# One core, AdaLN block with FNet and gMLP: modulation columns by VectorE products and ScalarE row sums, the small DFT matrices folded later, the first rows of y in two halves

## The chip, the core and the metric

The kernel runs on one core of a Trainium2 chip. The metric is the device time in microseconds of one launch, and lower is better. TensorE (PE in the profile), VectorE (DVE), ScalarE (ACT), GpSimd (POOL) and SyncE (SP) each take their own instructions in program order. Here SP issues nearly all loads, and POOL issues the stores, some small transfers and the loads of x for the residual.

## What is computed

```python
x = A_x                                             # 2048 x 512
mod = (_silu(c) @ w_mod).reshape(c.shape[0], 6, 1, -1)   # c: 1 x 512, w_mod: 512 x 3072
sa, ca, ga, sb, cb, gb = ...                        # six rows of 512
h = _layernorm(x, axis=-1) * (1 + ca) + sa
a = h @ dft_hid_re.T ; b = h @ dft_hid_im.T         # 512 x 512 matrices
x = x + ga * (dft_seq_re @ a - dft_seq_im @ b)      # 2048 x 2048 matrices
h = _layernorm(x, axis=-1) * (1 + cb) + sb
x = x + gb * _B_ref(h, ...)                         # gelu, layernorm, w_sp (2048 x 2048), w_out
```

All is float32. The change touches only the first half, up to the first writes of the new x.

## The kernel before

**Matmuls in three.** Each float32 product is made of three reduced-precision matmuls (`matmul3`, L83): a high part by a high part, a low part by the high one, and the high one by a low part. ACT makes a high part by a copy, DVE makes the low part by a subtraction.

**Stage A.** The kernel does not form `a` and `b`. It multiplies the two sequence matrices by the normalised x first, and the small hidden matrices (called ht) afterwards, with the modulation folded into them. Stage A runs over 128 chunks, here called steps n. One step is 128 columns of 512 rows of a sequence matrix, against one tile s of 128 normalised rows of x: 12 matmuls of 128x512 (`mm_a`, L342). In quarter t = 0 the steps alternate in fours between the real matrix (j = 0) and the imaginary one (j = 1), so that tile s = 4 is first used at step 8, s = 8 at step 16 and s = 12 at step 24. Quarter 0 ends with step 31.

**The order of the work.** A table made with `at(n, function, ...)` says which extra work is emitted behind step n (L627 to L720). Each step is emitted as `prep(n)` (L151), `mm_a(n)`, and then the extra work in the order in which it was entered. `prep(n)` has DVE transpose chunk n+3 (tile `t`, L147), ACT copy its high part (`ah`, L170), and DVE make the low part of chunk n+2 (`al`, L179). There are two buffers of `t`, four of `ah` and three of `al`. So `al` of chunk n+2 waits until PE has finished step n-1, and DVE cannot run more than about two steps ahead of PE. A block of a sequence matrix (tile `stage`, 1 MB, four steps) is loaded by SP into one of two buffers.

**Normalising x.** Tiles 0 to 3 have their statistics from DVE (`stats_x`). For tiles 4 to 15 ACT sums a row (`sum_x`, L302), sums the squares at the next step (`square_x`, L307) and normalises at the one after (`norm_x`, L108), with small POOL operations on the sums between (L303, L308 to L310). `hi_h` (ACT, tile `hh`, L325) and `lo_h` (DVE, tile `hl`, L330) split the result one step later. `norm_x` also writes ones into the first column by a small ACT copy (L317).

**Folding the modulation.** Three things are needed from the modulation in stage A: the shift sa and the scale 1 + ca as columns (512 numbers over partitions), and ga as a row (`mod2`). For the columns, w_mod is loaded (`wm`, `load_mod`); POOL multiplies and adds its four pieces (`weigh_mod`, L228, L230); DVE transposes and reduces (`turn_mod` L236, `column_mod` L241); POOL writes the result to DRAM and reads it back in four pieces (L243, L247). The folding then takes, for each of the two ht matrices: a load (`load_ht`, tile `hraw`), four transposes (`turn_ht`), POOL products and sums with the shift column (`weigh_ht`, L385 and L387), a first row that goes through DRAM to be spread over partitions (`load_w0`, L375 and L377, `scale_w0` L380), a scaling (`fold_ht` L403), and the split (`make_ht`, `make_ht_lo`). All this sits between steps 1 and 40.

**Rows of y.** `mm_y(t, i)` (L421) multiplies 128 rows of the result of stage A by ht: 24 matmuls. For quarter 0 it runs behind steps 44, 45, 46 and 46; `post_y` (L430) applies `mod2`, adds x, stores and takes the statistics.

Of the kernel before, what the change touches and what calls it, by code (L numbers as in the profile page):

```python
# [8 lines left out]
F32 = mybir.dt.float32  # L9
# [10 lines left out]
def fnet_gmlp_kernel(  # L20
# [50 lines left out]
    def bank(k, name):  # L71
        return psum.tile([P, 512], F32, tag=f"bank{k}", bufs=1, name=name)
# [131 lines left out]
    def load_mod(j):  # L204
        if j < 3:
            wm[j] = [spool.tile([P, D], F32, tag=f"wm{k}", bufs=1, name=f"wm{j}_{k}") for k in range(ND)]
        else:
            w = hpre.tile([P, ND, D], F32, tag="hraw", bufs=1, name=f"wm{j}")
            wm[j] = [w[:, k, :] for k in range(ND)]
        for k in range(ND):  # L210
            nc.sync.dma_start(wm[j][k], w_mod[k * P:(k + 1) * P, j * D:(j + 1) * D])
# [13 lines left out]

    def weigh_mod(j, k):
        w = wm[j]
        nc.gpsimd.tensor_scalar(w[k], w[k], sc[:, k:k + 1], 1.0, op0=ALU.mult, op1=ALU.mult)  # L228
        if k:
            nc.gpsimd.tensor_tensor(w[0], w[0], w[k], op=ALU.add)  # L230

    part, COL = {}, {}

    def turn_mod(j):
        part[j] = rows.tile([P, D], F32, tag="row", bufs=6, name=f"part{j}").rearrange("p (b i) -> p b i", i=32)
        nc.vector.transpose(part[j], wm.pop(j)[0].rearrange("p (b i) -> p b i", i=32))  # L236

    def column_mod(j):

        some = spool.tile([P, 16], F32, tag="some", bufs=2, name=f"some{j}")  # L240
        nc.vector.reduce_sum(some, part.pop(j), axis=mybir.AxisListType.X)  # L241
        d = dram.tile([P, 16], F32, name=f"some_d{j}")
        nc.gpsimd.dma_start(d, some)  # L243
        four = htpool.tile([P, 5, 4], F32, name=f"four{j}")
        v = d.rearrange("(c i) (a k) -> a i c k", i=32, k=4)
        for a in range(4):
            nc.gpsimd.dma_start(four[32 * a:32 * a + 32, :4, :], v[a])  # L247
        if j:
            nc.gpsimd.dma_start(four[:, 4, :], d.rearrange("(c i) b -> i b c", i=32)[0, 0].partition_broadcast(P))
        COL[j] = four  # L250

    def add_columns(j):
        four = COL[j]
        col = COL[j] = htpool.tile([P, 5], F32, name=f"col{j}")
        nc.vector.reduce_sum(col[:, :4], four[:, :4, :].rearrange("p c k -> p k c"), axis=mybir.AxisListType.X)
        if j:
            nc.vector.reduce_sum(col[:, 4:5], four[:, 4:5, :], axis=mybir.AxisListType.X)
            nc.vector.tensor_scalar(col, col, 1.0, None, op0=ALU.add)
            COL[2] = htpool.tile([P, 5], F32, name="col2")
            nc.vector.tensor_scalar(COL[2], col, -1.0, None, op0=ALU.mult)  # L260

# [6 lines left out]
    def split_mod(j):  # L268
        w = wm[j][0]
        wm[j] = [rows.tile([P, D], F32R, tag="row", bufs=6, name=f"ws{j}_{i}") if j == 2 else  # L270
                 hpre.tile([P, D], F32R, tag=f"ht{1 + i}", bufs=1, name=f"ws{j}_{i}") for i in range(2)]
        split(*wm[j], w)
# [40 lines left out]
    def norm_x(s):  # L313
        if s not in LN:
            LN[s] = spool.tile([P, D], F32, tag="xn", bufs=4, name=f"xn{s}")
        apply(LN[s], X.pop(s), NRM.pop(s))
        nc.scalar.activation(LN[s][:, 0:1], ones[:, 0:1], AF.Copy)  # L317

# [4 lines left out]
    def hi_h(s):  # L323
        h_hi[s] = hpool.tile([P, ND, P], F32R, name=f"hh{s}")
        nc.scalar.activation(*parts_h(s, h_hi), AF.Copy)  # L325

    def lo_h(s):
# [3 lines left out]
        LN.pop(s)  # L331

    def split_h(s):
        hi_h(s)
        lo_h(s)

# [34 lines left out]
    W0, ACC, QP = {}, {}, {}  # L371

    def load_w0(j):

        nc.gpsimd.dma_start(hrow_d[j], HR[j, 0][0:1, :])  # L375
# [3 lines left out]
    def scale_w0(j):  # L379
        nc.vector.tensor_scalar(W0[j], W0[j], COL[1 + j][:, 4:5], None, op0=ALU.mult)  # L380
# [30 lines left out]

    def make_ht_lo(j, k, eng=nc.vector):
        ht_lo[j, k] = htpool.tile([P, D], F32R, name=f"htl{j}_{k}")
        eng.tensor_tensor(ht_lo[j, k], HR.pop((j, k)), ht_hi[j, k].bitcast(F32), op=ALU.subtract)

# [4 lines left out]

    def mm_y(t, i):  # L421
        ps = YP[t, i] = bank(6 + i % 2, f"yp{t}_{i}")
        for j in range(2):
            for k in range(ND):
                gh, gl = gt_hi[t, j, k], gt_lo[t, j, k]
                cols = slice(i * P, (i + 1) * P)
                matmul3(ps, gh[:, cols], gl[:, cols], ht_hi[j, k], ht_lo[j, k],
                        j == 0 and k == 0, j == 1 and k == ND - 1)

    def post_y(t, i):  # L430
        x2 = X[t, i]
        y = rows.tile([P, D], F32, tag="y", bufs=1, name=f"y{t}_{i}")
        nc.vector.tensor_tensor(y, YP.pop((t, i)), mods[2], op=ALU.mult)
        nc.vector.tensor_tensor(x2, y, x2, op=ALU.add)  # L434
        nc.gpsimd.dma_start(x2_d[t][i * P:(i + 1) * P, :], x2)  # L435
        NRM[t, i] = norm([x2], "y")
# [192 lines left out]
    at(1, lo_h, 3)  # L629
    at(1, load_mod, 1)  # L630
    at(4, load_x, 2)
    at(12, load_x, 3)
    begin = [2, 3, 4, 5, 9, 10, 12, 13, 16, 18, 20, 21]
    for s, n in zip(range(4, NS), begin):
        at(n, sum_x, s)
        at(n + 1, square_x, s)
        at(n + 2, norm_x, s)
        at(n + 3, split_h, s)
    for k in range(ND):
        at((6, 7, 8, 9)[k], weigh_mod, 1, k)  # L640
        at((13, 14, 15, 16)[k], weigh_mod, 0, k)
        at((12, 13, 14, 15)[k], turn_ht, 0, k)
        at((22, 23, 24, 24)[k], weigh_ht, 0, k)
        at((25, 25, 26, 26)[k], fold_ht, 0, k)
    at(10, turn_mod, 1)
    at(11, column_mod, 1)
    at(10, load_mod, 0)
    at(11, load_ht, 0)
    at(15, add_columns, 1)
    at(16, load_w0, 0)  # L650
    at(16, load_ht, 1)
    at(17, turn_mod, 0)
    at(18, column_mod, 0)
    at(18, load_mod, 2)
    at(20, scale_w0, 0)
    at(21, add_columns, 0)
    at(23, sum_mod, 2, [0, 1])
    at(24, sum_mod, 2, [2, 3])
    at(25, split_mod, 2)

# [6 lines left out]
    at(26, change_pools)  # L667
    at(26, split_acc, 0)
    at(29, spread_mod, 2, 3, htpool, False)
    at(30, spread_acc, 0, 2)  # L670
    at(30, row_ht, 0)
    for i, k in enumerate((1, 2, 3, 0)):
        n = (26, 27, 28, 31)[i]
        at(n, make_ht, 0, k)
        at(n + 1, make_ht_lo, 0, k)
    for k in range(ND):
        at((29, 29, 30, 30)[k], turn_ht, 1, k)
        at((30, 31, 32, 33)[k], weigh_ht, 1, k)
        at((34, 35, 35, 36)[k], fold_ht, 1, k)
    at(30, load_w0, 1)  # L680
    at(33, scale_w0, 1)
    at(34, split_acc, 1)
    at(36, spread_acc, 1, 7)
    at(36, row_ht, 1)
    for i, k in enumerate((1, 2, 3, 0)):
        n = (36, 37, 38, 39)[i]
        at(n, make_ht, 1, k)
        at(n + 1, make_ht_lo, 1, k, nc.gpsimd if k else nc.vector)
    at(42, load_mod, 4)
    for j, n, k, plus_one in ((4, 48, 6, True), (3, 56, 7, False), (5, 64, 6, False)):  # L690
        at(n, sum_mod, j, [0, 1])
        at(n + 1, sum_mod, j, [2, 3])
        at(n + 2, split_mod, j)
        at(n + 4, spread_mod, j, k, cpool if j == 5 else htpool, plus_one)
        if j < 5:
            at(n + 4, load_mod, 5 if j == 3 else 3)
    for t in range(NQ):
        n = 8 * NQ * (t + 1)
        for i in range(4):
            y = N2 - 1 if t == NQ - 1 else (44, 45, 46, 46)[i] if t == 0 else n + 1 + 3 * i  # L700
            if i < 2:
                at(y - 4, load_xr, t, i)
# [152 lines left out]
```

## Time and profile before

| | |
|---|---|
| time, median of 3 runs (lowest to highest) | 1021.5 us (1020.74 to 1021.58) |
| the profiled execution: its time, and its span | 1021.03 us, 1019.2 us |
| TensorE clock granted over the span | 0.992 of full |
| busy: PE, weight loads, DVE, ACT, POOL | 98%, 80%, 53%, 31%, 18% |
| DMA | 114.85 MB, mean 113 GB/s |

The span runs from the first to the last instruction of the program; the time holds 1.8 us more. All places in the trace are microseconds from the start of the span. A matmul's duration overlaps the next one's, so PE's rate is read from the number of matmuls in a stretch. Step 0 of stage A begins at 11.25 us, and its last step ends at about 458 us.

### The profile page before, as it was taken

The page shows a single profiled execution, that of the slowest core. Times are in us where ns is not written, and L with a number is a line of the kernel's source. Part 1 is how long each engine was busy: PE and PEld are TensorE (multiplying, and loading weights), DVE is VectorE, ACT ScalarE, POOL GpSimd, SP SyncE. Part 2 cuts the span into 40 slices and gives each one's busy share as a digit, 9 for nine tenths or more (in the row PEclk, how much of TensorE's full clock was granted, in tenths as well). Part 3 has the DMA queues.
Part 4 walks back from the last instruction along what each step waited for, and adds up shares of the span by engine and source line. Part 5 has one row for each costly group of instructions (what it writes and reads, how often), then busy time and mean ns, then how long its engine had stood idle before and what let it go on. Part 6 is the DMA issues. An engine that isn't in the chain of part 4 may idle for free.

```text
span 1019.2 us, 11695 instructions
## 1 busy us (share of the span) xinstructions
PE 995.1 (98%) x4346; PEld 820.3 (80%) x4346; DVE 535.6 (53%) x800; ACT 313.5 (31%) x518; POOL 186.3 (18%) x316
## 2 busy tenths in 40 slices
PE   8977899999999999999999999999999999999998
PEld 5865688788888888888888999888888888888886
DVE  6664984578455554655543477555332532262325
ACT  5745441233132321331444477421111111111101
POOL 2654351104220032103312111101100200020002
PEclk9988999999999999999999999999999999999999
DMA  9985364266535443673745223324424322522131
GB/s 208 211 172 123 85 142 115 77 151 176 133 104 124 83 95 99 137 149 93 211 147 197 73 42 70 85 84 124 110 66 128 79 62 63 155 52 62 42 135 42
DMA packets 146538, 114.85 MB, mean 113 GB/s; under 512 B 7440, under 2 KB 126256, under 8 KB 146480
## 3 DMA queue, kind: packets, MB, share of 16 engines
q1 hardware_dynamic: 139296, 93.61, 39.4%
q0 software_dynamic: 6656, 20.49, 5.8%
q8 instruction: 34, 0.56, 0.3%
q14 instruction: 24, 0.20, 0.1%
q10 hardware_dynamic: 528, 0.00, 0.0%
HBM read 94.13 MB, written 19.94 MB: 112 GB/s over the span
## 4 chain that ended last, share of the span: by engine, by line
PE 87%; DVE 4%; DMA 3%; ACT 2%; POOL 2%; issue 1%; SPq 1%; DVEq 0%; ACTq 0%; POOLq 0%
PE gw L84 10%; PE gw L86 10%; PE gw L85 10%; PE gp L85 9%; PE gp L86 8%; PE gp L84 8%; PE yp L85 3%; PE yp L84 3%; PE yp L86 3%; PE z2p L85 3%; PE z2p L84 3%; PE z2p L86 3%; PE z1p L84 2%; PE z1p L85 2%; PE z1p L86 2%; PE op L86 2%
## 5 line engine op out<-in xcount | busy, mean ns | idle before, releaser
L170 ACT ACTIVATE ah<-t 128x512 fp32r<-128x512 f32 x224 | 141.4, 631 | 551.3 <-PE gw L86 214.2
L179 DVE TENSOR_TENSOR al<-t,ah 128x512 fp32r<-128x512 f32 x224 | 158.5, 708 | 270.5 <-PE gw L85 140.2
L85 PE MATMUL gp<-al,hh 128*128 128x512 f32 x512 | 203.2, 397 | 14.3 <-DVE al L179 14.3
L84 PE MATMUL gp<-ah,hh 128*128 128x512 f32 x512 | 202.4, 395 | 4.2 <-ACT ah L170 4.2
L86 PE MATMUL gp<-ah,hl 128*128 128x512 f32 x512 | 201.9, 394 | 0.1
L86 PE MATMUL gw<-ah,zl 128*128 128x512 f32 x448 | 174.3, 389 | 0.0
L85 PE MATMUL gw<-al,zh 128*128 128x512 f32 x448 | 174.3, 389 | 0.0
L84 PE MATMUL gw<-ah,zh 128*128 128x512 f32 x448 | 174.3, 389 | 0.0
L147 DVE STREAM_TRANSPOSE t<-stage 128x512 f32<-128x512 f32 x208 | 146.4, 704 | 7.3 <-DMA stage<-in_A_dft_seq_re_dram 4.3
L85 PEld LDWEIGHTS gp<-al,hh 128*128 128x128 f32 x512 | 97.7, 191 | 38.7 <-DVE al L179 18.5
L84 PEld LDWEIGHTS gp<-ah,hh 128*128 128x128 f32 x512 | 97.5, 190 | 26.6 <-ACT ah L170 5.5
L86 PEld LDWEIGHTS gp<-ah,hl 128*128 128x128 f32 x512 | 97.8, 191 | 21.2 <-DVE hl L330 0.8
L86 PEld LDWEIGHTS gw<-ah,zl 128*128 128x128 f32 x448 | 84.1, 188 | 17.6
L85 PEld LDWEIGHTS gw<-al,zh 128*128 128x128 f32 x448 | 84.1, 188 | 17.5
L84 PEld LDWEIGHTS gw<-ah,zh 128*128 128x128 f32 x448 | 84.1, 188 | 17.3
L564 POOL TENSOR_TENSOR u<-u,g 128x512 f32<-128x512 f32 x16 | 21.4, 1339 | 336.1 <-DVE g L562 336.1
L84 PE MATMUL yp<-hth,gh 128*128 128x512 f32 x128 | 50.6, 395 | 0.0
L85 PE MATMUL yp<-htl,gh 128*128 128x512 f32 x128 | 50.6, 395 | 0.0
L86 PE MATMUL yp<-hth,gl 128*128 128x512 f32 x128 | 50.5, 394 | 0.0
L435 POOL DMA_DIRECT2D x_d<-xr x16 | 8.8, 548 | 211.9 <-DVE xr L434 211.7
L85 PE MATMUL z2p<-wil,ah 128*128 128x448 f32 x128 | 46.7, 365 | 0.0
L84 PE MATMUL z2p<-wih,ah 128*128 128x448 f32 x128 | 46.7, 365 | 0.0
(127 smaller groups left out, 1197.2 us busy)
## 6 DMA issues: line engine op xcount, KB each, us to landing
stage<-in_A_dft_seq_re_dram SPq DMA_DIRECT2D x64, 256.0 KB, 4.8
stage<-in_A_dft_seq_im_dram SPq DMA_DIRECT2D x64, 256.0 KB, 5.3
stage<-in_B_w_sp_dram SPq DMA_DIRECT2D x64, 256.0 KB, 4.8
stage<-h_d SPq DMA_DIRECT2D x32, 256.0 KB, 4.6
z_d<-z POOLq DMA_DIRECT2D x28, 256.0 KB, 5.9
u<-z_d SPq DMA_DIRECT2D x4, 1792.0 KB, 8.0
wm<-in_w_mod_dram SPq DMA_DIRECT2D x24, 256.0 KB, 6.5
xr<-in_A_x_dram POOLq DMA_DIRECT2D x16, 256.0 KB, 3.5
```

The source lines that it names most:

```text
L84: nc.tensor.matmul(acc, ah, bh, start=first, stop=False)
L85: nc.tensor.matmul(acc, ah, bl, start=False, stop=False)
L86: nc.tensor.matmul(acc, al, bh, start=False, stop=last)
L147: nc.vector.transpose(dst.rearrange("p (b i) -> p b i", i=32), block[:, :, 32 * k:32 * k + 32])
L170: nc.scalar.activation(AH[n], T[n], AF.Copy)
L179: nc.vector.tensor_tensor(AL[n], T.pop(n), AH[n].bitcast(F32), op=ALU.subtract)
L435: nc.gpsimd.dma_start(x2_d[t][i * P:(i + 1) * P, :], x2)
L564: eng.tensor_tensor(U[t][:, f, :], U[t][:, f, :], g, op=ALU.mult)
```

## The change

1. **Columns of the modulation.** The block of w_mod is loaded with the same pattern as a sequence block, so that a DVE transpose brings its columns onto partitions. DVE multiplies by silu(c), which is spread over all partitions, and ACT sums along rows with its accumulator. There are eight such pieces (j, k): the scale (j = 1) behind steps 12, 13, 16, 18, and the shift (j = 0) behind 19, 20, 21, 23, each sum one step later. The product tile `wt` has one buffer. The POOL sums, the transposes of partial sums and the trip through DRAM go.
2. **The folding** is moved to later steps and spread: ht 0 is loaded at step 19, turned at 24 to 27, weighed at 29 and 30 by DVE (not POOL), folded at 34 to 36 and split at 35 to 39; ht 1 comes at 28 to 49. The first row is scaled as one row by ACT, stored one step later and read back spread five steps after the scaling. `mod2` moves from steps 18 to 29 to steps 41 to 53, and the other rows of the modulation follow it.
3. **y of quarter 0** is made in two halves: the real part behind steps 41, 42, 43, 45, copied to SBUF by ACT (`keep_y`), the imaginary part behind 54, 56, 58, 60, with one more DVE addition in `post_y`. y of quarter 1 begins behind step 72 instead of 65.
4. **x.** The second half of x tiles 4 to 7 is loaded behind step 0, not ahead of it. Tiles 4 to 7 have their statistics from DVE, at steps 4 and 6. For tiles 4 to 15 the ones are written by POOL. `lo_h` is emitted one step after `hi_h`.

```diff
-    def weigh_mod(j, k):
-        w = wm[j]
-        nc.gpsimd.tensor_scalar(w[k], w[k], sc[:, k:k + 1], 1.0, op0=ALU.mult, op1=ALU.mult)
-        if k:
-            nc.gpsimd.tensor_tensor(w[0], w[0], w[k], op=ALU.add)
...
-        d = dram.tile([P, 16], F32, name=f"some_d{j}")
-        nc.gpsimd.dma_start(d, some)
...
+    def load_columns(j):
+        pl, tag = (hpre, "hraw") if j else (spool, "wb")
+        WB[j] = pl.tile([P, 16, P], F32, tag=tag, bufs=1, name=f"wb{j}")
+        load_block(WB[j], quad(w_mod, 0, j))
+        COL[j] = htpool.tile([P, ND], F32, name=f"col{j}")
+
+    def weigh_column(j, k):
+        WT[j, k] = spool.tile([P, D], F32, tag="wt", bufs=1, name=f"wt{j}_{k}")
+        squares(WT[j, k], WB[j], k)
+        nc.vector.tensor_tensor(WT[j, k], WT[j, k], WB["c"], op=ALU.mult)
+
+    def sum_column(j, k):
+
+        w = WT.pop((j, k))
+        nc.scalar.activation(w, w, AF.Copy, accum_out=COL[j][:, k:k + 1])
+
+    def scale_columns():
+        col = COL[1]
+        nc.vector.tensor_scalar(col, col, 1.0, None, op0=ALU.add)
+        COL[2] = htpool.tile([P, ND], F32, name="col2")
+        nc.vector.tensor_scalar(COL[2], col, -1.0, None, op0=ALU.mult)
...
-        nc.scalar.activation(LN[s][:, 0:1], ones[:, 0:1], AF.Copy)
+        if s < 4:
+            nc.scalar.activation(LN[s][:, 0:1], ones[:, 0:1], AF.Copy)
+        else:
+            nc.gpsimd.memset(LN[s][:, 0:1], 1.0)
...
-        d = rows.tile([P, D], F32, tag="row", bufs=6, name=f"acc{j}_{k}")
-        nc.gpsimd.tensor_scalar(d, HR[j, k], COL[0][:, k:k + 1], 1.0, op0=ALU.mult, op1=ALU.mult)
-        if k:
-            nc.gpsimd.tensor_tensor(d, ACC[j], d, op=ALU.add)
-        ACC[j] = d
+        col = COL[0][:, k:k + 1]
+        if k == 0:
+            ACC[j] = rows.tile([P, D], F32, tag="row", bufs=6, name=f"acc{j}")
+            nc.vector.tensor_scalar(ACC[j], HR[j, k], col, None, op0=ALU.mult)
+        else:
+            nc.vector.scalar_tensor_tensor(ACC[j], HR[j, k], col, ACC[j], op0=ALU.mult, op1=ALU.add)
...
+    def keep_y(t, i):
+
+        Y0[t, i] = rows.tile([P, D], F32, tag="row", bufs=6, name=f"y0_{t}_{i}")
+        nc.scalar.activation(Y0[t, i], YP.pop((t, i)), AF.Copy)
...
-    begin = [2, 3, 4, 5, 9, 10, 12, 13, 16, 18, 20, 21]
-    for s, n in zip(range(4, NS), begin):
+    for s, n in ((4, 4), (5, 4), (6, 6), (7, 6)):
+        at(n, stats_x, s)
+        at(n + 1, norm_x, s)
+        at(n + 2, hi_h, s)
+        at(n + 3, lo_h, s)
+    for s, n in zip(range(8, NS), (10, 11, 12, 13, 18, 19, 20, 21)):
...
+    for j, ns in ((1, (12, 13, 16, 18)), (0, (19, 20, 21, 23))):
+        for k, n in enumerate(ns):
+            at(n, weigh_column, j, k)
+            at(n + 1, sum_column, j, k)
```

Three places show what moves. The first is POOL between the square sums of tiles 12 and 13 (`sums12`, `sums13`), before: products of w_mod (`wm0`), then the first row of ht (`hrow_d0`, `w0_0`), and the DRAM trip of the column (`some_d0`, `four0`).

```order
L303 TENSOR_SCALAR sums12_749<-sums12_749 128x1
L228 TENSOR_SCALAR wm0_3_542<-wm0_3_542,sc_109 128x512
L230 TENSOR_TENSOR wm0_0_539<-wm0_0_539,wm0_3_542 128x512
L375 DMA hrow_d0_113<-ht0_0_624 16x1x32
L377 DMA w0_0_755<-hrow_d0_113 128x512
L308 TENSOR_SCALAR sums12_749<-sums12_749 128x1
L309 TENSOR_TENSOR sums12_749<-sums12_749,mhalf_107 128x1
L310 TENSOR_TENSOR sums12_749<-sums12_749 128x1
L303 TENSOR_SCALAR sums13_807<-sums13_807 128x1
L243 DMA some_d0_812<-some0_810 128x16
L247 DMA four0_814<-some_d0_812 32x4x4 x4
```

The same place on POOL now, where `xn12` is the normalised tile into which the ones are written.

```order
L295 TENSOR_SCALAR sums12_765<-sums12_765 128x1
L300 TENSOR_SCALAR sums12_765<-sums12_765 128x1
L301 TENSOR_TENSOR sums12_765<-sums12_765,mhalf_107 128x1
L302 TENSOR_TENSOR sums12_765<-sums12_765 128x1
L295 TENSOR_SCALAR sums13_799<-sums13_799 128x1
L312 MEMSET xn12_764 128x1
L300 TENSOR_SCALAR sums13_799<-sums13_799 128x1
```

No product and no transfer stands between the small operations any more.

The second place is DVE from chunk 22's transpose on, before: `part0` and `some0` are the old column's reduction, `w0_0` the scaled first row, `hl12` and `hl13` low parts of x tiles.

```order
L147 STREAM_TRANSPOSE t22_827<-stage5_590 128x512
L179 TENSOR_TENSOR al21_831<-t21_786,ah21_788 128x512
L330 TENSOR_TENSOR hl12_847<-xn12_748,hh12_845 128x512
L147 STREAM_TRANSPOSE t23_853<-stage5_590 128x512
L179 TENSOR_TENSOR al22_862<-t22_827,ah22_829 128x512
L380 TENSOR_SCALAR w0_0_755<-w0_0_755,col1_715 128x512
L147 STREAM_TRANSPOSE t24_883<-stage6_725 128x512
L179 TENSOR_TENSOR al23_887<-t23_853,ah23_855 128x512
```

The same place on DVE now, with the products `wt0_0` and `wt0_1` of the shift's columns (`wb0` is the block of w_mod, `crow` the spread silu(c)) and the two small scalings of the scale's column (`col1`, `col2`).

```order
L147 STREAM_TRANSPOSE t22_771<-stage5_571 128x512
L179 TENSOR_TENSOR al21_775<-t21_746,ah21_748 128x512
L147 STREAM_TRANSPOSE wt0_0_803<-wb0_486 128x512
L242 TENSOR_TENSOR wt0_0_803<-wt0_0_803,crow_295 128x512
L147 STREAM_TRANSPOSE t23_806<-stage5_571 128x512
L179 TENSOR_TENSOR al22_815<-t22_771,ah22_773 128x512
L147 STREAM_TRANSPOSE wt0_1_840<-wb0_486 128x512
L242 TENSOR_TENSOR wt0_1_840<-wt0_1_840,crow_295 128x512
L251 TENSOR_SCALAR col1_388<-col1_388 128x4
L253 TENSOR_SCALAR col2_844<-col1_388 128x4
L147 STREAM_TRANSPOSE t24_846<-stage6_699 128x512
L179 TENSOR_TENSOR al23_850<-t23_806,ah23_808 128x512
```

Between two pairs of `t` and `al` there now stand a transpose and a product. The transpose of `wt0_1` writes the one buffer of `wt`, so it waits for the ACT sum of `wt0_0`.

The third place is ACT over the same steps, before: one part each of the work for x tiles 12, 13 and 14.

```order
L170 ACTIVATE ah23_855<-t23_853 128x512
L108 ACTIVATE xn13_806<-x3_609,sums13_807 128x512
L317 ACTIVATE xn13_806<-ones_105 128x1
L302 ACTIVATE xn14_878,sums14_879<-x3_609 128x512
L170 ACTIVATE ah24_885<-t24_883 128x512
L325 ACTIVATE hh13_901<-xn13_806 128x512
L307 ACTIVATE xn14_878,sums14_879<-x3_609,sums14_879 128x512
```

The same place on ACT now, where `wt0_0` and `wt0_1` are the row sums.

```order
L170 ACTIVATE ah23_808<-t23_806 128x512
L108 ACTIVATE xn12_764<-x3_590,sums12_765 128x512
L299 ACTIVATE xn13_798,sums13_799<-x3_590,sums13_799 128x512
L294 ACTIVATE xn14_835,sums14_836<-x3_590 128x512
L247 ACTIVATE wt0_0_803,col0_491<-wt0_0_803 128x512
L170 ACTIVATE ah24_848<-t24_846 128x512
L320 ACTIVATE hh12_864<-xn12_764 128x512
L108 ACTIVATE xn13_798<-x3_590,sums13_799 128x512
L299 ACTIVATE xn14_835,sums14_836<-x3_590,sums14_836 128x512
L294 ACTIVATE xn15_872,sums15_873<-x3_590 128x512
L247 ACTIVATE wt0_1_840,col0_491<-wt0_1_840 128x512
```

Two to three operations per chunk have become four to five, since the work on tiles 12 to 15 now begins at four steps in a row (18, 19, 20, 21), and each row sum stands last behind them.

More of the change, by code (lines that the diff above doesn't have):

```diff
@@ L204, in load_mod @@
     def load_mod(j):
[L205 to L209, printed above, removed]
+        w = hpre.tile([P, ND, D], F32, tag="hraw", bufs=1, name=f"wm{j}")
+        wm[j] = [w[:, k, :] for k in range(ND)]
         for k in range(ND):
@@ L224, in sum_mod @@
                 nc.vector.scalar_tensor_tensor(w[0], w[k], sc[:, k:k + 1], w[0], op0=ALU.mult, op1=ALU.add)
-    def weigh_mod(j, k):
-        w = wm[j]
-        nc.gpsimd.tensor_scalar(w[k], w[k], sc[:, k:k + 1], 1.0, op0=ALU.mult, op1=ALU.mult)
-        if k:
[L230 to L236, printed above, removed]
@@ L238, in column_mod @@
-    def column_mod(j):
-        some = spool.tile([P, 16], F32, tag="some", bufs=2, name=f"some{j}")
-        nc.vector.reduce_sum(some, part.pop(j), axis=mybir.AxisListType.X)
-        d = dram.tile([P, 16], F32, name=f"some_d{j}")
-        nc.gpsimd.dma_start(d, some)
[L244 to L260, printed above, removed]
+    WB, WT, COL = {}, {}, {}
@@ new lines, in load_row, with silu_row @@
+    def load_row():
+        WB["c"] = rows.tile([P, D], F32, tag="row", bufs=6, name="crow")
+        nc.sync.dma_start(WB["c"], c[0].partition_broadcast(P))
+    def silu_row():
+        nc.scalar.activation(WB["c"], WB["c"], AF.Silu)
+    def load_columns(j):
[3 more added lines that the diff above has]
+        COL[j] = htpool.tile([P, ND], F32, name=f"col{j}")
@@ L269, in split_mod @@
         w = wm[j][0]
-        wm[j] = [rows.tile([P, D], F32R, tag="row", bufs=6, name=f"ws{j}_{i}") if j == 2 else
-                 hpre.tile([P, D], F32R, tag=f"ht{1 + i}", bufs=1, name=f"ws{j}_{i}") for i in range(2)]
+        wm[j] = [hpre.tile([P, D], F32R, tag=f"ht{1 + i}", bufs=1, name=f"ws{j}_{i}") for i in range(2)]
         split(*wm[j], w)
@@ L419, in load_xr, with mm_y @@
         nc.gpsimd.dma_start(X[t, i], x[o:o + P, :])
-    def mm_y(t, i):
-        ps = YP[t, i] = bank(6 + i % 2, f"yp{t}_{i}")
-        for j in range(2):
+    def mm_y(t, i, js=(0, 1)):
+        ps = YP[t, i] = bank(6 + i % 2, f"yp{t}_{i}_{js[0]}")
+        for j in js:
             for k in range(ND):
@@ L606, in fnet_gmlp_kernel @@
     load(1)
-    load_x(1)
+    load_x(1, range(2))
     keep_busy(7, 5)
@@ L629, in fnet_gmlp_kernel @@
     at(1, lo_h, 3)
-    at(1, load_mod, 1)
+    at(0, load_x, 1, range(2, 4))
+    at(2, load_row)
+    at(9, silu_row)
     at(4, load_x, 2)
+    at(5, load_columns, 1)
+    at(8, load_columns, 0)
     at(12, load_x, 3)
-    begin = [2, 3, 4, 5, 9, 10, 12, 13, 16, 18, 20, 21]
-    for s, n in zip(range(4, NS), begin):
+    at(19, load_ht, 0)
+    at(28, load_ht, 1)
+    for s, n in ((4, 4), (5, 4), (6, 6), (7, 6)):
[4 more added lines that the diff above has]
+    for s, n in zip(range(8, NS), (10, 11, 12, 13, 18, 19, 20, 21)):
         at(n, sum_x, s)
@@ L637, in fnet_gmlp_kernel @@
         at(n + 2, norm_x, s)
[L638 to L659, printed above, removed]
+        at(n + 3, hi_h, s)
+        at(n + 4, lo_h, s)
+    for j, ns in ((1, (12, 13, 16, 18)), (0, (19, 20, 21, 23))):
+        for k, n in enumerate(ns):
+            at(n, weigh_column, j, k)
+            at(n + 1, sum_column, j, k)
+    at(20, scale_columns)
     def change_pools():
```

86 lines of the change are left out of this document (43 added, 43 removed).

## Prediction

> **What bounds the kernel now.** I read the page first, then busy time by stretches, then the chain of waits.
>
> ```profile
> span 1019.2 us, 11695 instructions
> PE 995.1 (98%) x4346; PEld 820.3 (80%) x4346; DVE 535.6 (53%) x800; ACT 313.5 (31%) x518; POOL 186.3 (18%) x316
> ```
>
> PE is busy nearly throughout, and the change leaves the number of matmuls as it is. So it can only win where PE stands still. The stretches of 20 us show where. Their first number with an x is the count of matmuls, then come DVE, ACT, POOL, the granted clock and the DMA rate.
>
> ```profile
> 20.00:40.00 20.00, 20.00 (x89) 16.25 (x88) 13.84 (x21) 16.18 (x37) 9.30 (x20) 1.00 1.12 238
> 40.00:60.00 20.00, 15.52 (x66) 12.51 (x65) 9.86 (x16) 9.38 (x21) 10.44 (x18) 0.93 0.92 195
> 60.00:80.00 20.00, 18.92 (x75) 15.09 (x74) 14.26 (x23) 9.48 (x21) 11.08 (x18) 0.89 0.77 153
> 80.00:100.00 20.00, 14.87 (x54) 11.09 (x53) 8.66 (x15) 12.30 (x28) 9.51 (x23) 0.83 0.47 117
> 100.00:120.00 20.00, 15.32 (x58) 11.61 (x57) 19.08 (x27) 8.27 (x16) 7.21 (x6) 0.91 0.26 56
> 120.00:140.00 20.00, 19.62 (x86) 15.85 (x86) 19.29 (x30) 8.53 (x16) 9.21 (x9) 1.00 0.52 117
> 180.00:200.00 20.00, 18.57 (x81) 14.85 (x80) 8.77 (x16) 4.17 (x7) 3.58 (x9) 1.00 0.12 40
> ```
>
> An undisturbed stretch has 89 matmuls, so one takes 20/89 = 0.225 us and a step of twelve 2.70 us. The other six rows lack 23, 14, 35, 31, 3 and 8 matmuls. Together that is 114 x 0.225 = **25.6 us**, and it is all that this change can recover: the start, ahead of 20 us, keeps its order, and behind 200 us PE is full.
>
> The chain says what PE waits for there. Its columns are start, length and work.
>
> ```profile
> 40.51 1.71 POOL wm L230
> 44.88 0.72 DVE part L236
> 48.98 7.51 DMA hraw<-in_A_dft_hid_re_dram
> 56.51 0.71 DVE ht L147
> 58.45 0.79 PE gp L85
> ...
> 73.77 6.57 DMA hrow_d<-ht
> 82.46 0.82 ACT xn L108
> 88.13 5.63 DMA four<-some_d
> ```
>
> First POOL's weighing of w_mod is late, so the transpose that frees its buffer is late, so SP issues the load of ht late, and DVE stands in front of ht's transpose with PE's chunk behind it. Then POOL stands in front of two DRAM round trips, and the small operations on the sums behind them hold up ACT's normalisation. From 100 us on it is DVE itself, at 19 of 20 us.
>
> Part of the loss is the clock. These rows are narrower stretches, and one PE row with the idle time before it.
>
> ```profile
> 60.80:64.20 3.40, 3.40 (x10) 2.63 (x9) 2.59 (x5) 3.05 (x9) 2.50 (x5) 0.50 1.00 203
> 105.10:108.60 3.50, 0.95 (x4) 0.49 (x3) 3.46 (x6) 1.15 (x2) 2.27 (x2) 1.00 0.69 132
> 108.60:112.00 3.40, 3.40 (x9) 2.67 (x8) 3.40 (x7) 1.35 (x3) 0.00 (x0) 0.50 0.02 5
> 108.06 0.50 PE L85 MATMUL gp<-al,hh 128*128 128x512 f32 x1 [2.55 <-DVE al L179]
> ```
>
> After 2.55 us of idle PE the clock was granted at 0.50 for 3.4 us, which costs 1.7 us more. The Trainium skill, in "TensorE: Matmul & The Clock Gate", section "HAM oscillation — how this bites in real kernels", names idle gaps above about 3.4 us as the thing to avoid. Here 2.55 us sufficed, so the measurement decides. By the page's number the stall that I forecast below would carry no clock cost, and the sum would be 1.7 us lower.
>
> **The change, part by part.** *What goes.* POOL's products, the three DRAM trips on POOL's queue ahead of the sums, and ht's load and transposes go from steps 6 to 19, or move behind them. This removes every link quoted from 40 to 94 us. The DVE load of 100 to 140 us (`mod2`, folding and splitting of both ht in a dozen steps) is spread to step 53, partly beside y's extra matmuls. The stall in 180:200 came from `post_y` packed behind step 46; now it stands two steps apart, each time behind twelve more matmuls. I count all 25.6 us as removed, and then add what is new.
>
> *Loads.* By the SP order, up to the stage block of step 20, 10.25 MB are now issued where it was 11 MB. At 238 GB/s in the first row that is no worse than before, and each block should land two or more microseconds ahead of its transpose. I take 0. If one came 1 to 2 us late, DVE's lead of two steps would cover it.
>
> *Statistics of tiles 4 to 7 on DVE.* Two at step 4 and two at step 6 add, from the rows below, 2 x (0.73 + 0.18) = 1.8 us to a step in which DVE has 1.4 us free (2.70 - 0.63 - 0.65) after its transpose and low part. The step between is free, so it evens out. I take 0, at most +1; a small gain is possible too, since ACT loses two operations per tile.
>
> *The eight column pieces.* Here I expect the new stall. ACT's issue at full load in the trace of before:
>
> ```profile
> 28.31 0.61 ACT L170 ACTIVATE ah<-t 128x512 fp32r<-128x512 f32 x1
> 28.83 0.62 ACT L325 ACTIVATE hh<-xn 128x512 fp32r<-128x512 f32 x1
> 29.35 0.80 ACT L108 ACTIVATE xn<-x,sums 128x512 f32<-128x512 f32 x1
> 30.18 0.20 ACT L317 ACTIVATE xn<-ones 128x1 f32<-128x1 f32 x1
> 30.29 0.71 ACT L307 ACTIVATE xn<-x,sums 128x512 f32<-128x512 f32 x1
> 30.91 0.19 ACT L307 ACTIVATION_READ_ACCUMULATOR xn<-x,sums 128x1 f32 x1
> 31.00 0.62 ACT L302 ACTIVATE xn<-x 128x512 f32<-128x512 f32 x1
> 31.52 0.19 ACT L302 ACTIVATION_READ_ACCUMULATOR xn<-x 128x1 f32 x1
> 31.61 0.62 ACT L170 ACTIVATE ah<-t 128x512 fp32r<-128x512 f32 x1
> ```
>
> From start to start: `ah` 0.52, `hh` 0.52, squares 0.71, a row sum 0.61 (0.71 until its accumulator is read, 31.00 to 31.71). Normalising took 0.83 with the ones waiting on it; now nothing of ACT does, and by the pattern of the others (0.1 under their length) I take 0.71. DVE's rows, the last two of them for the small column scalings:
>
> ```profile
> 26.39 0.71 DVE L147 STREAM_TRANSPOSE t<-stage 128x512 f32<-128x512 f32 x1 [1.35 <-DMA stage<-in_A_dft_seq_re_dram]
> 27.02 0.65 DVE L179 TENSOR_TENSOR al<-t,ah 128x512 fp32r<-128x512 f32 x1
> ...
> 194.35 0.69 DVE L434 TENSOR_TENSOR xr<-y,xr 128x512 f32<-128x512 f32 x1
> 195.08 0.69 DVE L92 BATCH_NORM_STATS2 bsty<-xr 128x6 f32<-128x512 f32 x1
> 195.81 0.18 DVE L94 BATCH_NORM_AGGREGATE mvy<-bsty 128x2 f32<-128x6 f32 x1
> ...
> 66.89 1.18 DVE L258 TENSOR_SCALAR col<-col 128x5 f32<-128x5 f32 x1
> 68.10 0.63 DVE L260 TENSOR_SCALAR col<-col 128x5 f32<-128x5 f32 x1
> ```
>
> A piece costs DVE 0.73 (the product must wait for its transpose, as in the step from 194.35 to 195.08) + 0.61 = 1.34 us. That alone fits a step: 1.34 + 0.63 + 0.65 = 2.6 of 2.70. But `wt` has one buffer. A piece waits for ACT's sum of the last one, that sum stands last behind a step's ACT work, and this begins with `ah`, which needs the `t` that DVE transposes behind the last piece. So two pieces in adjacent steps go in a circle: piece 1.34, `t` until `ah` 0.80 (its 0.71 and the handing over), `ah` 0.52, normalising 0.71, squares 0.71, sum 0.61, row sum 0.71: 5.4 us, and 0.52 more where `hh` is in it, against 2.70 for PE.
>
> Call the start of step 19 zero. The row sum of piece (1,3) ends at the earliest at 2.6: `ah`, squares, sum and row sum. Worked through by the same intervals from step 12 it is 4.0, since pieces (1,2) and (1,3), with the low parts of tiles 10 and 11 between them, put DVE 1.4 us behind. I take 4.0. Piece (0,1) may then begin at 4.0 + 5.4 = 9.4. `al` of chunk 23 follows it by 1.34, the two small scalings (0.4, as the aggregate's 0.18 twice; at most the 1.81 of the last two rows), 0.63 and 0.65: 12.4. PE needs it as the second matmul of step 23, at 4 x 2.70 + 0.2 = 11.0: **1.4 us**. Piece (0,2) begins at 9.4 + 5.4 + 0.4 + 0.52 = 15.7. `al` of chunk 24 is ready at 15.7 + 1.34 + 0.63 + 0.65 = 18.3, and `hl` of tile 12, queued behind it, at 18.95. PE, now at 14.9, wants them at 15.1 and 15.35: **3.6 us**. Piece (0,3) has a step in between, and DVE catches up. In the earlier group (12, 13, 16, 18) the slack of two steps holds: by the same sum chunk 16 is ready 1.5 us ahead of PE.
>
> So 5.0 us of new waits around 75 to 85 us; 3.6 with the early start, 6.4 with slow scalings. The second wait exceeds 2.55 us, so I add 1.7 for the clock: 0 if it is not cut, 3.4 if it is cut for 6.8 us. Behind ACT's waiting `ah`, what stands late is tile 12's `hh` and the later sums; nobody but PE waits for them.
>
> *Folding, y and the rest.* At steps 27, 39 and 47 DVE's queue is fullest; counted at 0.65 per operation, the lead is used up and nothing left over: 0, at most +1.5. y's halves add one DVE operation of 0.7 per 128 rows beside twelve matmuls, 0.
>
> **The sum.** 1021.0 (the profiled execution's time) - 25.6 + 5.0 + 1.7 = 1002.1. The median of the runs is 0.5 higher than that execution, and so is the forecast: **1002.6 us**.
>
> **Rivals.**
> - *The circle is hidden.* If ACT gets through faster than start to start in the trace of before, or DVE's lead at step 19 is larger, the waits vanish: 1021.5 - 25.6 = 996, down to 994 if ACT's relief helps the early steps. Against it: every link is an in-order queue or one buffer. For it: 5.0 us rests on a lag of a few microseconds built up over twelve steps. Chance 0.22.
> - *More of the same.* Handing over costs 0.1 more per link and the clock stays cut for 6.8 us (the row up to 64.20 is the second half of such a stretch), or a transfer lands late, or steps 27 to 31 add their 1.5: 6.4 + 3.4 + 1.5 = 11.3, so 1007, up to 1012. Chance 0.17.
> - *Slower than before.* The circle never opens. If the early group has no slack either, each of the eight pieces costs PE a circle less one step, 5.4 + 0.4 - 2.7 = 3.1 us, and each such gap can halve the clock: 8 x (3.1 + 1.7) = 38 us, so 1034. It decides as soon as `al` of chunk 16 comes later than PE's step 16; by my sum it comes 1.5 us before. Chance 0.04.
> - *The change does not do what it says*: the waits of 40 to 94 us come back behind other transfers, near 1021. The queues show nothing that could do it. Chance 0.01.
>
> **How the numbers follow.** The forecast has 0.56, and by itself spans 998 to 1006: 3.6 to 6.4 us of waits, 0 to 3.4 us of clock and 1 us of loose ends. The range to 8 in 10 takes in most of the first two rivals: 995 to 1010. A difference of 0.2% (2 us) is about what a measurement of this kernel can tell from none. Faster: 0.56 + 0.22 + 0.17 = 0.95; same 0.01; slower 0.04.
>
> **What would show it.** In the profile after, the stretches 40 to 140 us should have 85 or more matmuls each, except the one around 75 to 90 us, which lacks some 25 to 30. PE's two longest waits should be for `al` and `hl` there, with DVE's transpose of `wt` waiting for ACT's row sum just before, and a clock of 0.50 behind it. POOL's waits for DMA should be gone. The prediction is wrong if 75 to 90 us is full, or if PE waits for `stage`, `hraw` or the halves of y.

## The result and the profile after

The changed kernel takes **1002.9 us**, the median of four runs (1002.74 to 1003.07), against 1021.5 before: 0.982 of the time, with a 95% interval of 0.9803 to 0.9837. The forecast was 1002.6. The profiled execution took 1002.74 us, with a span of 1000.9, so 18.3 us less than the one before on either measure.

The first lines of the page of after:

```profile
span 1000.9 us, 11701 instructions
PE 989.3 (99%) x4346; PEld 818.9 (82%) x4346; DVE 543.6 (54%) x830; ACT 315.1 (31%) x513; POOL 142.3 (14%) x282
```

PE's busy time fell by only 6 us while the span fell by 18: what went is idle time of PE, and some matmuls at half the clock. The stretches of after show where some is left; they are those that the prediction read of before.

```profile
20.00:40.00 20.00, 20.00 (x90) 16.59 (x89) 17.20 (x31) 11.56 (x19) 5.30 (x16) 1.00 1.13 223
40.00:60.00 20.00, 20.00 (x90) 16.58 (x89) 13.51 (x21) 14.55 (x34) 4.85 (x19) 1.00 1.19 210
60.00:80.00 20.00, 18.85 (x83) 15.30 (x82) 12.48 (x22) 12.27 (x30) 3.20 (x13) 1.00 0.80 160
80.00:100.00 20.00, 17.05 (x67) 13.37 (x67) 17.99 (x30) 12.29 (x28) 3.42 (x10) 0.91 0.30 66
100.00:120.00 20.00, 20.00 (x89) 16.54 (x89) 18.44 (x31) 8.41 (x15) 0.00 (x0) 1.00 0.80 158
120.00:140.00 20.00, 20.00 (x89) 16.46 (x89) 16.29 (x27) 7.81 (x14) 1.07 (x2) 1.00 0.72 171
180.00:200.00 20.00, 20.00 (x88) 16.34 (x87) 14.15 (x24) 5.25 (x8) 4.38 (x10) 1.00 0.71 174
```

Five of the rows are full, with 88 to 90 matmuls. Two are not: 60 to 80 us lacks 6 of 89 and 80 to 100 us lacks 22, together 28 x 0.225 = 6.3 us. The waits of PE say for what, in all, how often, and the longest one:

```profile
PE gp L85 <- DVE al L179: 4.7, 4, 3.0
PE gp L84 <- ACT ah L170: 1.7, 1, 1.7
```

And its rows, with start, length and, in brackets, the idle time before:

```profile
11.35 0.49 PE L84 MATMUL gp<-ah,hh 128*128 128x512 f32 x1 [1.70 <-ACT ah L170]
...
77.66 0.50 PE L85 MATMUL gp<-al,hh 128*128 128x512 f32 x1 [1.15 <-DVE al L179]
...
83.63 0.66 PE L85 MATMUL gp<-al,hh 128*128 128x512 f32 x1 [2.95 <-DVE al L179]
84.23 0.80 PE L86 MATMUL gp<-ah,hl 128*128 128x512 f32 x1
```

The wait at 77.66 is for `al` of chunk 23, that at 83.63 for `al` of chunk 24, and the 0.60 us until the next matmul is `hl` of tile 12. The 1.7 us for `ah` is the wait that ends the start. Behind 83.8 us the clock is halved:

```profile
80.30:83.70 3.40, 0.45 (x3) 0.07 (x1) 2.72 (x5) 1.21 (x4) 0.64 (x3) 1.00 0.00 0
83.80:87.20 3.40, 3.40 (x8) 2.40 (x9) 3.04 (x6) 3.40 (x8) 1.12 (x4) 0.50 0.00 0
```

DVE's rows over these steps show the circle of the one buffer.

```profile
69.13 0.71 DVE L147 STREAM_TRANSPOSE wt<-wb 128x512 f32<-128x512 f32 x1 [2.12 <-ACT wt L247]
...
74.59 0.71 DVE L147 STREAM_TRANSPOSE wt<-wb 128x512 f32<-128x512 f32 x1 [2.83 <-ACT wt L247]
...
75.94 0.16 DVE L251 TENSOR_SCALAR col<-col 128x4 f32<-128x4 f32 x1
76.14 0.17 DVE L253 TENSOR_SCALAR col<-col 128x4 f32<-128x4 f32 x1
76.32 0.71 DVE L147 STREAM_TRANSPOSE t<-stage 128x512 f32<-128x512 f32 x1
...
80.94 0.71 DVE L147 STREAM_TRANSPOSE wt<-wb 128x512 f32<-128x512 f32 x1 [3.34 <-ACT wt L247]
```

ACT's rows between two of those pieces show what they waited for:

```profile
77.12 0.63 ACT L170 ACTIVATE ah<-t 128x512 fp32r<-128x512 f32 x1 [2.57 <-DVE t L147]
77.66 0.61 ACT L320 ACTIVATE hh<-xn 128x512 fp32r<-128x512 f32 x1
78.18 0.80 ACT L108 ACTIVATE xn<-x,sums 128x512 f32<-128x512 f32 x1
78.88 0.71 ACT L299 ACTIVATE xn<-x,sums 128x512 f32<-128x512 f32 x1
...
79.59 0.62 ACT L294 ACTIVATE xn<-x 128x512 f32<-128x512 f32 x1
...
80.20 0.61 ACT L247 ACTIVATE wt<-wt 128x512 f32<-128x512 f32 x1
80.72 0.19 ACT L247 ACTIVATION_READ_ACCUMULATOR wt<-wt 128x1 f32 x1
```

Read together: DVE stands for 2.83 us in front of the piece at 74.59, because ACT is still summing the last one; `t` at 76.32 stands behind that piece; ACT stands for 2.57 us in front of `ah`, because it needs that `t`; the row sum ends at 80.91, behind `ah` and four more operations; and at 80.94 the next piece begins. From piece to piece it is 5.46 and 6.35 us, where PE needs 2.72 for a step.

The chain of waits of after tells this place otherwise. Its rows, again start, length and work:

```profile
72.10 4.17 DMA stage<-in_A_dft_seq_im_dram
76.32 0.72 DVE t L147
```

By these `t` waited for a transfer that landed at 76.27. But by DVE's own rows the two small scalings ran until 76.31, and `t` follows at 76.32 in any case. Nor is it the block that this `t` reads. The `t` at 76.32 is chunk 24 and comes from `stage6`, a block of the real matrix, and SP issued that block's loads long before:

```profile
58.63 1.91 SPq L139 DMA_DIRECT2D stage<-in_A_dft_seq_re_dram  x4
```

The transfer in the chain is of the imaginary matrix. It fills the buffer that chunk 23, the `t` at 70.49, had just left, and it is itself late because that `t` was. The expectations of the experiments still have a late transfer as a rival of the circle.

### The profile page after: what moved, and what is told of

Its sections match the earlier page's. It is cut to its first block, busy times and chain, and to the rows that moved or that the text cites. A ratio compares the mean times of both kernels' runs of the same rounds, so it can differ in the third digit from the quotient of the medians.

```text
span 1000.9 us, 11701 instructions
## 1 busy us (share of the span) xinstructions
PE 989.3 (99%) x4346; PEld 818.9 (82%) x4346; DVE 543.6 (54%) x830; ACT 315.1 (31%) x513; POOL 142.3 (14%) x282
## 4 chain that ended last, share of the span: by engine, by line
PE 94%; DVE 2%; ACT 1%; DMA 1%; issue 1%; SPq 0%; DVEq 0%; ACTq 0%
PE gp L85 11%; PE gp L86 11%; PE gp L84 10%; PE gw L84 10%; PE gw L86 10%; PE gw L85 10%; PE yp L85 3%; PE yp L84 3%; PE yp L86 3%; PE z2p L85 3%; PE z2p L84 3%; PE z2p L86 3%; PE z1p L84 3%; PE z1p L85 3%; PE z1p L86 3%; PE op L86 2%
## 5 line engine op out<-in xcount | busy, mean ns | idle before, releaser
L179 DVE TENSOR_TENSOR al<-t,ah 128x512 fp32r<-128x512 f32 x224 | 153.1, 683 | 274.6 <-PE gw L85 143.0
L86 PE MATMUL z2p<-wih,al 128*128 128x448 f32 x128 | 46.8, 366 | 0.0
```

The costliest lines, as they stand in the source:

```text
L86: nc.tensor.matmul(acc, al, bh, start=False, stop=last)
L179: nc.vector.tensor_tensor(AL[n], T.pop(n), AH[n].bitcast(F32), op=ALU.subtract)
```

## The experiments

One number recurs: the time from the start of step 23 to that of step 25, in which both waits and the halved clock lie. It is 11.90 us in the changed kernel. In a kernel without a wait there it is 5.44, two steps of 2.72. Kernels were compared with the kernel before on the same chip, which took 1021.8 (the first four) and 1021.9 us (the others), where the chip of the result took 1021.5; so a few tenths between two kernels say nothing.

### Six buffers for the product

```diff
-        WT[j, k] = spool.tile([P, D], F32, tag="wt", bufs=1, name=f"wt{j}_{k}")
+        WT[j, k] = rows.tile([P, D], F32, tag="row", bufs=6, name=f"wt{j}_{k}")
```

> The products wt take the six-buffer row pool of which four are free at steps 12 to 24, so a piece no longer waits for ACT's row sum of the last piece; every engine's instructions and their order are those of the changed kernel (1002.9 us). Theory (the circle through the one buffer costs 1.3 + 3.1 us of waits at steps 23 and 24 and then 1.7 to 1.9 us of halved clock): the waits vanish and the time is 996.5, no halved clock behind 80 us. Rival (ACT simply has more work than a step holds at 19 to 22, so its copies are late whatever the buffer): 1001 to 1003, PE still waits at 23 and 24. Rival (the stage transfer that the chain of waits names in front of the transpose of step 21): 1003, unchanged.

It took 996.4 us (995.38 to 996.79), 0.9751 of the time before (0.9737 to 0.9764). Its two stretches around the place:

```profile
60.00:80.00 20.00, 20.00 (x89) 16.54 (x89) 18.51 (x32) 16.41 (x40) 6.64 (x19) 1.00 0.91 167
80.00:100.00 20.00, 20.00 (x90) 16.57 (x89) 18.04 (x29) 9.78 (x19) 1.40 (x3) 1.00 0.65 137
```

Both are full, the clock is whole, and steps 23 and 24 take 5.44 us. ACT has the same operations as in the changed kernel, so its load is not the cause. Against a late transfer this run says less than the rows above: SP issues each load behind one of DVE's transposes, and these come earlier when the circle goes. The one buffer cost 6.5 us.

### The row sum right behind `ah`

One buffer as in the changed kernel, but the row sums are registered ahead of the work on x, so that each stands second in its step on ACT and not last.

```diff
+    for j, ns in ((1, (12, 13, 16, 18)), (0, (19, 20, 21, 23))):
+        for k, n in enumerate(ns):
+            at(n + 1, sum_column, j, k)
     for s, n in zip(range(8, NS), (10, 11, 12, 13, 18, 19, 20, 21)):
...
             at(n, weigh_column, j, k)
-            at(n + 1, sum_column, j, k)
```

> One buffer as in the changed kernel, but each row sum stands right behind the step's copy ah on ACT, ahead of that step's normalising, squares and sums; the same instructions. Theory: the circle shortens from 5.4 to 5.9 us to 1.34 + 0.80 + 0.52 + 0.71 = 3.4 us, 0.7 us over a step, which DVE's lead of two steps absorbs for three adjacent pieces: 996.5, as with six buffers. Rival (ACT's load): same load, so 1001 to 1003. Rival (the transfer): 1003.

It took 996.4 us (995.86 to 996.64), 0.9751 (0.9738 to 0.9765), and the same two stretches are full:

```profile
60.00:80.00 20.00, 20.00 (x90) 16.58 (x89) 17.00 (x30) 16.00 (x39) 7.42 (x18) 1.00 0.87 161
80.00:100.00 20.00, 20.00 (x90) 16.56 (x89) 18.52 (x32) 10.70 (x21) 2.02 (x5) 1.00 0.68 145
```

Neither a buffer nor an operation was added or taken away. The circle needs both its halves, the one buffer and the sum's place behind ACT's other work; breaking either one gives back the same 6.5 us.

### The earlier pieces in adjacent steps

```diff
-    for j, ns in ((1, (12, 13, 16, 18)), (0, (19, 20, 21, 23))):
+    for j, ns in ((1, (15, 16, 17, 18)), (0, (19, 20, 21, 23))):
```

> The scale's pieces stand at steps 15, 16, 17, 18, directly ahead of the shift's at 19, 20, 21, 23, so that seven pieces follow in adjacent steps. Theory: the lag builds up earlier, by the same intervals to waits of 0.7, 3.1 and 3.7 us at steps 22, 23 and 24, 7.5 in place of 4.4 to 5, and one or two stretches of halved clock (1.7 or 3.4): 1006 to 1008. Rival (ACT's load at 19 to 22 alone, since the earlier pieces leave ACT's steps 13 and 14 and go to 16 to 18, where it has room): 1002 to 1003. Rival (the transfer): 1003.

It took 1004.3 us (1003.96 to 1005.72), 0.9832 (0.9819 to 0.9846): slower than the changed kernel, as the circle has it, but by 1.4 us, where at least 3 had been expected. PE's rows say where the rest went.

```profile
80.14 0.50 PE L85 MATMUL gp<-al,hh 128*128 128x512 f32 x1 [2.82 <-DVE al L179]
...
82.14 0.63 PE L84 MATMUL gp<-ah,hh 128*128 128x512 f32 x1
82.57 0.63 PE L85 MATMUL gp<-al,hh 128*128 128x512 f32 x1
...
86.11 0.50 PE L85 MATMUL gp<-al,hh 128*128 128x512 f32 x1 [1.37 <-DVE al L179]
```

The long wait now comes a step earlier, at step 23, and behind it the clock is halved: matmuls are 0.43 us apart. That slows PE by about 1.6 us on its way to step 24, where `al` is late anyway. So the wait there is 1.37 us and not 2.95. The waits and the clock's cost are not to be added when a late operand stands behind the halved stretch: PE would only have waited longer. The sign was right, the sum too big: steps 22 to 24 lost 7.8 us in all, and the expected waits alone were 7.5.

### Matmuls in the gap

Ten matmuls with a stationary tile of zeros stand behind step 23 on PE. They add work that changes nothing, zeros to a sum, and occupy PE while it would wait.

```diff
+        ZERO.append(rows.tile([P, D], F32R, tag="row", bufs=6, name="zero"))
+        nc.scalar.activation(ZERO[0], WB["c"], AF.Copy, scale=0.0)
...
+            nc.tensor.matmul(GP[0, 0, 0], ZERO[0][:, :P], h_hi[0].rearrange("p k i -> p (k i)"), start=False, stop=False)
...
+    at(23, pad, 10)
```

> Ten extra matmuls with a zero stationary tile are put behind step 23 on PE, 2.3 us at full clock, so that most of the wait of 3.1 us in step 24 is filled with work that changes nothing in the sum; ACT writes the zero tile at step 15. Theory that the halved clock is a cost of its own beside the wait: no halved clock near 84 us, 1002.9 - 1.9 = 1001.0. Rival (the clock falls whatever PE does there, or the extra matmuls delay step 24): 1002.9 or more.

It took 1001.8 us (1001.13 to 1001.89), 0.9803 (0.979 to 0.9817). A row of PE, the added ones, then the stretch behind the wait:

```profile
80.68 2.49 PE L668 MATMUL gp<-hh,zero 128*128 128x512 f32 x10
...
84.02 0.50 PE L85 MATMUL gp<-al,hh 128*128 128x512 f32 x1 [0.61 <-DVE al L179]
```

```profile
83.80:87.20 3.40, 3.08 (x12) 2.35 (x13) 3.07 (x6) 3.40 (x9) 1.00 (x4) 1.00 0.00 0
```

`al` comes no earlier (its matmul begins 7.50 us after step 23, where it was 7.51), but the clock stays at 1.00, and from step 23 to step 25 it is 10.50 us where it was 11.90. So the halved clock costs 1.4 us here. The prediction had 1.7, and the expectation of this run 1.9.

### The old columns in the changed kernel

POOL's products, the partial sums and the trip through DRAM return at the steps where they stood, and everything else of the change stays.

```diff
-    def weigh_column(j, k):
-        WT[j, k] = spool.tile([P, D], F32, tag="wt", bufs=1, name=f"wt{j}_{k}")
...
+    def weigh_mod(j, k):
+        w = wm[j]
+        nc.gpsimd.tensor_scalar(w[k], w[k], sc[:, k:k + 1], 1.0, op0=ALU.mult, op1=ALU.mult)
...
+        at((6, 7, 8, 9)[k], weigh_mod, 1, k)
+        at((13, 14, 15, 16)[k], weigh_mod, 0, k)
```

> The columns are made as before (POOL products at steps 6 to 9 and 13 to 16, DVE transposes and reductions, the trip through DRAM on POOL's queue at steps 11 and 18), the folding, y in halves, x and the later rows of the modulation as changed. The folding's share of the gain stays, the columns' share goes. Theory (POOL's products and its waits for DRAM hold up the sums of tiles 10 to 15, which ACT then waits for): PE waits again around steps 16 to 18 and 22 to 26, 5 to 12 us with halved clocks, in place of the circle through wt: 1002 to 1009. Rival (the gain came from the later folding alone: without ht's load, transposes and first row in the way, the old columns are hidden): 996 to 998.

It took 1004.7 us (1004.43 to 1005.31), 0.9832 (0.9818 to 0.9845). PE's waits (that for `ah` ends the start), the first link of the chain, and then rows of POOL, ACT and DVE:

```profile
PE gp L84 <- ACT hh L327: 2.5, 1, 2.5
PE gp L84 <- ACT ah L170: 2.3, 1, 2.3
PE gp L85 <- DVE al L179: 2.7, 2, 2.3
```

```profile
48.54 7.15 DMA some_d<-some
```

```profile
58.95 0.12 POOL L319 MEMSET xn<- 128x1 f32 x1
59.10 0.63 ACT L327 ACTIVATE hh<-xn 128x512 fp32r<-128x512 f32 x1 [7.97 <-POOL xn L319]
60.54 0.81 ACT L108 ACTIVATE xn<-x,sums 128x512 f32<-128x512 f32 x1 [0.81 <-POOL sums L309]
73.88 0.71 DVE L236 STREAM_TRANSPOSE part<-wm 128x512 f32<-128x512 f32 x1 [3.21 <-POOL wm L230]
```

Such links stood in the chain of before: the trip to DRAM takes 7.15 us while POOL stands in front of it, and later POOL's products hold up DVE. But what ACT waits for first, 7.97 us in front of `hh` of tile 8, are not that tile's sums. It is the ones in its first column, which the change writes by POOL and the kernel before wrote by ACT. The sums of tile 9 come late behind them. Steps 15 and 16 lose 4.2 us by this and step 20 loses 4.2 by the products, each with a halved clock behind its wait; at steps 23 and 24 there is no wait. So half of the loss comes from the old columns and the ones on POOL together, and what the old columns would cost without the latter was not tried. The later folding, y's halves and the rest without the new columns bring 1021.9 - 1004.7 = 17.2 us. The new columns add 8.3 us with the circle broken (1004.7 - 996.4) and 1.8 as they are in the change (1004.7 - 1002.9). New columns with the old folding were not tried, so this split holds for this order of the two parts.

### The old sums of x

On top of the six buffers, tiles 4 to 7 are loaded and summed as before: by ACT, which also writes the ones.

```diff
-    for s, n in ((4, 4), (5, 4), (6, 6), (7, 6)):
-        at(n, stats_x, s)
...
-    for s, n in zip(range(8, NS), (10, 11, 12, 13, 18, 19, 20, 21)):
+    for s, n in zip(range(4, NS), (2, 3, 4, 5, 10, 11, 12, 13, 18, 19, 20, 21)):
```

> The kernel with six buffers for wt (996.4 us), but tiles 4 to 7 are loaded ahead of step 0 and have their sums from ACT at steps 2 to 5, and ACT writes the ones, all as before the change. The prediction counted this part at nothing: 996.0 to 997.0. Rival (ACT's relief is what lets the column pieces through: 0.11 us more per tile at steps 18 to 22, and fuller early steps): waits at steps 4 to 8 or 22 to 24, 998 or more.

It took 996.7 us (996.27 to 997.15), 0.9753 (0.974 to 0.9766), against 996.4 with six buffers alone, and the ranges overlap. That part of the change is worth nothing that can be measured, as the prediction counted it.

### The three together

Six buffers, the row sum right behind `ah`, and two more of the matmuls that keep PE occupied before the first operands are there.

```diff
-    keep_busy(7, 5)
+    keep_busy(9, 5)
```

> Six buffers for wt, each row sum at the front of its step, and nine warm-up matmuls in place of seven ahead of step 0. In every trace of the changed kernels the warm-up ends 1.9 to 2.7 us before the first real matmul and the clock is halved for 3.4 us from 11 to 13 us on; in the trace of before the gap was 1.8 us and there was no halved clock, and steps 0 to 3 took 12.4 us from their start in place of 12.7 to 13.2. Theory (that gap halves the clock): without it steps 0 to 3 take 12.4, and the time is 995.4 to 996.0. Rival (the first steps wait for x and its statistics anyway): 996.4.

It took **995.7 us** (995.66 to 996.2, five runs), 0.9744 (0.9731 to 0.9757), the lowest median of all kernels here. All of PE's longer waits, the first one among the matmuls that only keep it occupied:

```profile
PE busyp L259 <- DVE busy L201: 1.5, 1, 1.5
PE gp L85 <- DVE al L179: 0.4, 1, 0.4
```

The 1.7 us for `ah` at the start is gone. The stretch from 14 to 16 us, first of the six-buffer kernel and then of this one, differs by the clock:

```profile
14.00:16.00 2.00, 2.00 (x6) 1.62 (x5) 2.00 (x4) 0.12 (x1) 1.65 (x3) 0.50 1.26 227
```

```profile
14.00:16.00 2.00, 2.00 (x11) 1.65 (x10) 1.97 (x5) 0.49 (x1) 1.29 (x3) 1.00 1.27 228
```

From step 0 to step 4 it is 12.42 us here and 13.13 there. The 0.7 us is about the spread of the runs (the lowest with six buffers alone was 995.38), so it is the traces that show it, not the times. The mean clock says the same: it was 0.999 or 1.000 in all five runs here, and 0.998 in three of the four with six buffers alone (a stretch of 3.4 us at half the clock takes 0.002 off the mean); the fourth, at 1.000, was the one of 995.38. But the run with the old sums of x, with seven warm-up matmuls, shows no halved clock at its start either, 1.12 us of idle time there and 12.39 us to step 4. So the two matmuls are not the only way to a full clock. (By the profile's idle times the gap is 1.28 to 2.15 us in the traces that the expectation speaks of, and 1.17 before; the expectation counts from the start of the last warm-up matmul.)

## Why the prediction was right, point by point

**What bounds the kernel.** That only PE's gaps could be won, 25.6 us of them, holds. Outside the one place the rows quoted of after are full, and with that place mended and nothing else the kernel stands at 996.4, where the rival "the circle is hidden" had put it (996).

**Counted at nothing.** Loads: nothing waits for `hraw`, and DVE waits for a `stage` once, at 9.92 us, ahead of step 0. The x sums are confirmed by a run of their own. Folding and y: of 100 to 280 us nothing is lost, and one wait of 0.4 us for `al` remains near 291 us. The small scalings were 0.16 and 0.17 us, 0.33 for 0.4.

**The circle.** It was 5.46 and 6.35 us, where 5.4 and 6.3 had been worked out from ACT's and DVE's intervals in the trace of before. The lag at step 19 was the doubtful number: piece (0,0) begins 3.9 us after that step, where the row sum ahead of it had been put at 4.0. The two waits of PE, less the 0.225 us that a matmul takes anyway, are 1.53 - 0.225 = 1.3 us at step 23 (1.4 predicted), and at step 24 3.34 + 0.60 less two of these, 3.5 (3.6 predicted). That the circle is the cause is shown twice, by more buffers and by another order; against the transfer that the chain names speak DVE's rows and the block that it fills.

**The clock** was one halved stretch of 3.4 us at this place, as forecast, at 1.4 us for 1.7.

**The sum.** Waits and clock together are 11.90 - 5.44 = 6.5 us (6.7 predicted). Two things were not foreseen. The start got slower, since `ah` of the first step came after 1.70 us of idle PE and the clock was halved there: from step 0 to step 4 13.09 us instead of 12.41, so 0.7 us. And there is the 0.4 us near 291 us. By the matmul counts, 25.6 - 6.3 - 0.7 - 0.4 = 18.2 us, against 18.3 between the two spans. The prediction had put the start at nothing because its order is kept. That is not quite so: the second half of x tiles 4 to 7 is loaded behind step 0. In the six traces with this order and seven warm-up matmuls, PE stands idle for 1.28 to 2.33 us ahead of step 0, and the clock is halved there; in the two with the old order, before and with the old sums of x, it is 1.17 and 1.12 us, and the clock stays whole. The order of these loads was not changed by itself, so the cause stays open.

For a profiled execution the forecast's sum gave 1002.1, and 1002.74 was measured: 1.1 us that were not foreseen, less the 0.4 by which the loss at the circle was smaller. The medians are only 0.3 apart, because the median lies 0.2 above the profiled execution where 0.5 had been added. That is luck of a few tenths.

**What would show it.** The place lacks 28 matmuls, where some 25 to 30 had been forecast. The longest wait of PE is there, for `al`, but the second longest, 1.70 us, is that of the start. POOL's waits for DMA should be gone. One is left, `w` for the first row of ht, which has five steps to spare:

```profile
POOL w L374 <- DMA hrow_d<-w0r: 3.3, 1, 3.3
```

PE waits for nothing behind it.

**The rivals.** "More of the same" fell with the clock, which was not halved twice at this place. "Slower than before" needed the early group of pieces without slack; in the changed kernel `al` of chunk 16 is done at 55.6, 1.7 us ahead of its matmul, where 1.5 had been worked out. Even with the pieces in adjacent steps the kernel stayed at 1004.3. There ACT has less other work at the first steps, the pieces begin 3.4 to 4.8 us apart and not 5.4, and DVE's lead takes up the difference until step 22. What is lost behind that is made smaller by the overlap of waits and halved clock, which the rival's price of 3.1 + 1.7 us a piece left out.

## What to carry to other kernels

A buffer with one copy ties its producer to the consumer's place in the consumer's queue: walk the circle once, with start-to-start intervals from the trace, and compare it with the step that has to hide it. If it is longer, moving the consumer forward in its queue is worth as much as more buffers (6.5 us either way here), and costs no memory. When the chain of waits names a transfer that landed just before an operation, look whether the engine was free at that time, and whether the operation reads that block at all, before you believe it.

## What the runs showed of the hardware

The clock of PE was halved after shorter idle times than had been thought. In the changed kernel it fell after 1.70 us (the start) and 2.95 us, and did not fall after 1.15 us (step 23). But the length of one gap does not decide it. In the run with adjacent pieces the clock fell at the start after 1.28 us, with 0.31 us more behind the first matmul, and stayed whole behind the 1.37 us at 86.11. Within each trace here the changes of the clock lie whole multiples of 3.41 us apart, so look at the 3.41 us just ahead of such a time, in that run at 12.24 and at 87.33 us:

```profile
8.83:12.24 3.41, 1.82 (x6) 0.64 (x5) 2.50 (x4) 2.57 (x5) 0.00 (x0) 1.00 1.13 256
83.92:87.33 3.41, 1.94 (x8) 1.07 (x7) 3.38 (x7) 1.75 (x3) 0.00 (x0) 1.00 0.00 0
```

PE is idle for 1.59 us of the first, and the clock is halved from 12.24 us on; it is idle for 1.47 us of the second, and the clock stays at 1.00. In the nine traces up to 140 us the clock fell from 1.00 each time that PE was idle for 1.59 us or more of such a stretch, and never at 1.47 us or less. No run was made to find the limit. The Trainium skill, in "TensorE: Matmul & The Clock Gate", section "HAM oscillation — how this bites in real kernels", puts the danger at gaps above about 3.4 us; here less than half of that sufficed, in two gaps.

In stage A each halved stretch of the changed kernel and of the experiments lasted 3.4 us. In the kernel before, two of the three lasted 6.8 us, from 57.4 and from 84.7 us.

A halved stretch behind a wait is cheaper than its matmuls suggest if another late operand follows: 1.4 us in the changed kernel, where half of 3.4 is 1.7, and next to nothing in the run with adjacent pieces, where PE would have waited in any case.
